# The 1e-9 of a softmax's row sums: one addition becomes a sum over two values, in three fixed tiles

## The chip, the cores and the metric

The kernel runs on one core of one Trainium2 chip. A core has five engines that work side by side, each through its own list of instructions in order: PE (TensorE, matmuls and transposes), DVE (VectorE), ACT (ScalarE), POOL (GpSimd) and SP (which issues most DMA transfers). They wait for each other by semaphores. The metric is the device time of the whole program in microseconds (us); lower is better.

## The reference

Three stages follow each other: attention with normalized queries and keys (4 batches, 12 heads, 448 tokens, head size 64), a mixture of experts in which each of 1792 tokens goes to one of 8 experts, and a dense layer with a sigmoid GELU. The change concerns the end of the softmax alone:

```python
scores = scores - np.max(scores, axis=-1, keepdims=True)
attn = np.exp(scores)
attn = attn / (np.sum(attn, axis=-1, keepdims=True) + 1e-09)
return np.matmul(attn, v).astype(np.float32)
```

## The kernel before

**Attention.** The 48 heads run one after the other, software-pipelined. The 448 tokens of a head are 4 chunks of 112 partitions. `qk` (L218) multiplies two chunks at a time into a PSUM tile `S`; `top` (L229, DVE) takes the negated row maxima into a small tile `sm`; `ex` (L236, ACT) forms the exponentials `A` and, in the same instruction, their row sums, also into `sm`. `at` (L245, PE) transposes `A` into a PSUM tile `pA` with two buffers, which ACT (L252) or DVE (L254) copies out; `avu` (L265, PE) multiplies with V for a pair of heads. The division is done late: `finish_pair` (L274 to L279) copies the product out, adds 1e-9 to the 8 row sums per partition of the pair (L278) and takes their reciprocals `rinv` (L279). One head later `xtok` (L289, PE) transposes the product into the PSUM tile `tp`, of which there is one buffer, and `put_x` (L301, DVE) multiplies it with `rinv`. The transposes of the next queries (L184) and keys (L199) use the same single `tp` buffer, as do the gate's products (L314, L325, read by DVE at L328 and L335).

**The order.** It is written out by hand: the list `ORDER` names the steps of one head, and the scheduler leaves them so. In it `FP` is `finish_pair`, done at every second head as the last step but the gate's, directly before the next head's `top` on DVE; `XP` is `put_x`, at the other heads. `S4` is a step of a weight conversion that runs beside the attention: each step is one DVE instruction (L896 or L901, in turn) with two SBUF inputs, directly ahead of `FP` or `XP`.

**POOL's part.** Once for four heads it prepares queries and keys of a later group: `norm` (12 small operations, L159 to L162, then L164 and two of L167), `split` (L172), and `squares` of the group after (L131 and the foldings L136, L137 for q, then for k). DVE sums what it folded (L142, L146) and gives it the start of the next group's norm (L151).

**After the attention** come the routing, then four pairs of experts, each with its share of the dense layer.

```python
"K0 M0 A0 A1 C1 P3 C0 TQ CQ E0 K1 A2 TK M1 A3 CK C3 C2 AV P0 LK E1 S4 XT P1 P2 FP XP GA GB S5"
```

Of the kernel before, what the change touches and what calls it, by code (L numbers as in the profile page):

```python
# [20 lines left out]
FT = mybir.dt.float32  # L21
# [5 lines left out]
OP = mybir.AluOpType  # L27
AX = mybir.AxisListType
# [23 lines left out]
class Attn:  # L52


    def __init__(s, ctx, tc, q, k, v, g_q, g_k, w_gate, consts, xd, logits):
        s.tc, s.nc = tc, tc.nc
        s.q, s.k, s.v = q, k, v
        s.B, s.H, s.S, s.D = q.shape
        s.C, s.NC = 112, 4
        s.identf, s.identr = consts["identf"], consts["identr"]  # L60
        s.xd, s.logits = xd, logits
        nc = s.nc
        ep = lambda name, bufs=1: ctx.enter_context(tc.tile_pool(name=name, bufs=bufs))
        s.cst = ep("a_cst")
        s.io = ep("a_io", 2)
        s.wk = ep("a_wk", 2)
        s.ps = ctx.enter_context(tc.tile_pool(name="a_ps", bufs=1, space=bass.MemoryType.PSUM))
        s.groups, s.of = [], {}
        for b in range(s.B):
            h = b * s.H  # L70
            for n in ([2, 2, 4, 4] if b == 0 else [4, 4, 4]):
                for i in range(n):
                    s.of[h + i] = (len(s.groups), i)
                s.groups.append((h, n))
                h += n
        s.grp, s.nbuf, s.nsmall = {}, 0, 0
        s.load(0, "qk")
        s.gk = s.cst.tile([128, 2], FT, name="gk")
        for hh in range(2):
            for j, g in enumerate((g_q, g_k)):  # L80
                nc.scalar.dma_start(s.gk[hh * 64:(hh + 1) * 64, j:j + 1],
                                    bass.AP(tensor=g.tensor, offset=g.offset, ap=[[1, 64], [1, 1]]))
        s.load(0, "v")
        s.load(1)
        s.load(2)
        s.wg0 = s.cst.tile([128, 6, 8], FT, name="wg0")
        nc.scalar.dma_start(s.wg0, w_gate.rearrange("(c p) e -> p c e", p=128))
        s.A, s.sums, s.qT, s.khi, s.klo, s.AT, s.xuT, s.rinv, s.av = {}, {}, {}, {}, {}, {}, {}, {}, {}
        s.Sp, s.pA, s.sumsp = {}, {}, {}

    def params(s):
        nc = s.nc
        s.G = s.cst.tile([128, 1], FT, name="G")
        nc.vector.scalar_tensor_tensor(s.G, s.gk[:, 0:1], 1.0 / math.sqrt(s.D), s.gk[:, 1:2],
                                       op0=OP.mult, op1=OP.mult)
# [116 lines left out]
    def qk(s, h, u):  # L212
        nc = s.nc
        p = s.ps.tile([128, 2, 512], FT, name="S", bufs=2)[:112]
        for c in range(2):
            i = 2 * u + c
            for n, mv in enumerate((s.khi[h], s.klo[h])):
                nc.tensor.matmul(p[:, c, 0:448], s.qT[h][:, i, :], mv.rearrange("p i t -> p (i t)"),  # L218
                                 start=(n == 0), stop=(n == 1))
        if u == 0:  # L220
            s.A[h] = s.wk.tile([112, 4, 448], FT, name="A", bufs=2)
            if h % 2 == 0:
                s.sums2 = s.wk.tile([112, 4, 2, 2], FT, name="sm", bufs=3)
                s.sumsp[h // 2] = s.sums2[:, :, 1]
            s.sums[h] = s.sums2[:, :, :, h % 2]
        s.Sp[u] = p

    def top(s, h, u):
# [39 lines left out]
    def finish_pair(s, pr):  # L268
        nc = s.nc
        b, pl = divmod(pr, 6)  # L270
        if pl == 0:
            s.rinv[b] = s.wk.tile([112, 4, 12], FT, name="rinv", bufs=2)
        xu = s.wk.tile([128, 448], FT, name="xu", bufs=5)
        nc.scalar.copy(xu, s.av[pr])  # L274
        s.xuT[pr] = xu
        ri = s.rinv[b]
        o = ri[:, :, 2 * pl:2 * pl + 2]
        nc.vector.tensor_scalar(o, s.sumsp[pr], 1e-9, None, op0=OP.add)  # L278
        nc.vector.reciprocal(o, o)  # L279

    def xtok(s, pr, end=False):
# [1045 lines left out]
```

## Time and profile before

| | us |
|---|---|
| runs shown | 1264.83, 1273.66, 1274.99 (median 1273.66) |
| the profiled execution | 1265.38 |
| its span, first to last instruction | 1263.6 |
| busy: PE, DVE, POOL, ACT | 1141.4, 875.3, 705.1, 659.2 |
| L278, busy in all | 19.4, in 24 instructions |

Busy time is what an engine spends from the start to the end of its instructions; an instruction that is held up after it began counts as busy for the whole of that. The chain of waits follows the work that ended last back from instruction to instruction.

### The profile page before, as it was taken

The page shows a single profiled execution, that of the slowest core. Times are in us where ns is not written, and L with a number is a line of the kernel's source. Part 1 is how long each engine was busy: PE and PEld are TensorE (multiplying, and loading weights), DVE is VectorE, ACT ScalarE, POOL GpSimd, SP SyncE. Part 2 cuts the span into 40 slices and gives each one's busy share as a digit, 9 for nine tenths or more (in the row PEclk, how much of TensorE's full clock was granted, in tenths as well). Part 3 has the DMA queues.
Part 4 walks back from the last instruction along what each step waited for, and adds up shares of the span by engine and source line. Part 5 has one row for each costly group of instructions (what it writes and reads, how often), then busy time and mean ns, then how long its engine had stood idle before and what let it go on. Part 6 is the DMA issues. An engine that isn't in the chain of part 4 may idle for free.

```text
span 1263.6 us, 19388 instructions
## 1 busy us (share of the span) xinstructions
PE 1141.4 (90%) x6952; PEld 961.0 (76%) x6952; DVE 875.3 (69%) x1525; ACT 659.2 (52%) x1289; POOL 705.1 (56%) x588
## 2 busy tenths in 40 slices
PE   4999999999967777879999999999999899999995
PEld 3666666667536676768988898988989799899995
DVE  7799999999789878698657936447885533781100
ACT  4888888888643245654234545224544323555420
POOL 3788677784344546446645674565455355554552
PEclk9899999999967888899998999999999999999998
DMA  6454454423124379864336643436643343763421
GB/s 174 117 145 110 127 152 116 139 76 89 33 74 105 104 206 285 269 220 149 103 110 194 189 127 110 130 106 185 196 130 104 101 124 119 209 190 112 135 78 33
DMA packets 185504, 172.95 MB, mean 137 GB/s; under 512 B 9536, under 2 KB 159808, under 8 KB 185408
## 3 DMA queue, kind: packets, MB, share of 16 engines
q1 hardware_dynamic: 180080, 160.55, 44.0%
q0 software_dynamic: 4224, 11.14, 2.9%
q8 instruction: 55, 0.90, 0.3%
q14 instruction: 41, 0.34, 0.1%
q10 hardware_dynamic: 1104, 0.03, 0.0%
HBM read 147.96 MB, written 23.72 MB: 136 GB/s over the span
## 4 chain that ended last, share of the span: by engine, by line
PE 63%; DVE 23%; issue 6%; DMA 3%; ACT 2%; POOL 2%; SPq 0%; POOLq 0%; DVEq 0%; ACTq 0%
PE mm L1025 11%; PE mm L1026 11%; PE mm L1027 11%; PE mm L1036 5%; PE S L218 5%; PE pA L245 5%; PE av L265 4%; PE mm L1037 3%; DVE gs L1082 2%; DVE B L565 2%; DVE wc L901 2%; DVE B L567 2%; DVE tt L1078 1%; DMA xg<-xd,idx 1%; DVE wc L896 1%
## 5 line engine op out<-in xcount | busy, mean ns | idle before, releaser
L964 POOL TENSOR_TENSOR wlo<-raw,whi 128x768 fp32r<-128x768 f32 (+1 forms) x175 | 385.5, 2205 | 380.9 <-ACT whi L961 362.9
L961 ACT CAST whi<-raw 128x768 fp32r<-128x768 f32 (+1 forms) x224 | 207.0, 924 | 145.6 <-issue 50.8
L1025 PE MATMUL mm<-gs,whi 128*128 128x448 f32 (+1 forms) x432 | 159.4, 369 | 0.5 <-DVE zs L1075 0.5
L1026 PE MATMUL mm<-gs,whi 128*128 128x448 f32 (+1 forms) x432 | 155.9, 361 | 0.0
L1027 PE MATMUL mm<-gs,wlo 128*128 128x448 f32 (+1 forms) x432 | 155.8, 361 | 0.0
L1025 PE MATMUL mm<-zs,whi 128*128 128x448 f32 x384 | 144.1, 375 | 4.6 <-ACT whi L961 4.6
L1027 PE MATMUL mm<-zs,wlo 128*128 128x448 f32 x384 | 142.6, 371 | 5.3 <-POOL wlo L964 3.6
L1026 PE MATMUL mm<-zs,whi 128*128 128x448 f32 x384 | 142.1, 370 | 0.9 <-DVE zs L1084 0.9
L236 ACT ACTIVATE A<-S,sm 112x448 f32<-112x448 f32 x192 | 122.5, 658 | 12.6 <-DVE sm L229 12.6
L1036 PE MATMUL mm<-gs,whi 128*128 128x448 f32 x336 | 110.7, 385 | 10.1 <-DVE gs L1082 10.1
L229 DVE TENSOR_REDUCE sm<-S 112x2 f32<-112x896 f32 x96 | 104.1, 1085 | 19.3 <-PE S L218 18.2
L1036 PE MATMUL mm<-xs,whi 128*128 128x448 f32 x336 | 111.9, 389 | 0.1
L245 PE MATMUL pA<-ident,A 112*112 112x112 f32 x768 | 99.8, 264 | 9.3 <-DVE AT L254 9.1
L245 PEld LDWEIGHTS pA<-ident,A 112*112 112x112 f32 x768 | 84.0, 136 | 22.3 <-DVE AT L254 11.0
L1097 DVE TENSOR_TENSOR gs<-sg,gs 128x448 fp32r<-128x448 f32 x64 | 42.2, 661 | 81.9 <-ACT gs L1096 81.8
L1025 PEld LDWEIGHTS mm<-gs,whi 128*128 128x128 f32 x432 | 83.5, 193 | 10.7 <-issue 4.3
L1095 ACT ACTIVATE sg<-mm 128x448 f32<-128x448 f32 x64 | 34.8, 543 | 103.9 <-PE mm L1027 103.9
L1027 PEld LDWEIGHTS mm<-gs,wlo 128*128 128x128 f32 x432 | 83.4, 193 | 6.2
L1026 PEld LDWEIGHTS mm<-gs,whi 128*128 128x128 f32 x432 | 83.5, 193 | 5.7
L1037 PE MATMUL mm<-xs,wlo 128*128 128x224 f32 x336 | 83.4, 276 | 4.3 <-POOL spacer L1134 1.9
L1037 PE MATMUL mm<-gs,wlo 128*128 128x224 f32 x336 | 83.8, 270 | 1.0 <-DVE wlo L964 1.0
L218 PE MATMUL S<-khi,qT 128*112 128x448 f32 x192 | 79.2, 412 | 4.9 <-ACT khi L206 4.9
(228 smaller groups left out, 2632.6 us busy)
## 6 DMA issues: line engine op xcount, KB each, us to landing
raw<-in_moe_w_dram SPq DMA_DIRECT2D x64, 384.0 KB
raw<-in_moe_w_dram SPq DMA_DIRECT2D x48, 512.0 KB
raw<-din SPq DMA_DIRECT2D x64, 384.0 KB
raw<-dout SPq DMA_DIRECT2D x48, 512.0 KB
r<-in_moe_w_in_dram SPq DMA_DIRECT2D x24, 512.0 KB
r<-in_moe_w_out_dram SPq DMA_DIRECT2D x24, 512.0 KB
din<-wc SPq DMA_DIRECT2D x24, 256.0 KB
dout<-wc SPq DMA_DIRECT2D x48, 128.0 KB
```

Of the source, the lines that this page charges most:

```text
L218: nc.tensor.matmul(p[:, c, 0:448], s.qT[h][:, i, :], mv.rearrange("p i t -> p (i t)"), start=(n == 0), stop=(n == 1))
L229: s.nc.vector.tensor_reduce(s.sums[h][:, 2 * u:2 * u + 2, 0], s.Sp[u][:, :, 0:448], axis=AX.X, op=OP.max, negate=True)
L236: s.nc.scalar.activation(s.A[h][:, i, :], p[:, c, 0:448], AF.Exp, bias=sm[:, i, 0:1], scale=1.0, accum_out=sm[:, i, 1:2])
L245: nc.tensor.transpose(p[:, qc], s.A[h][:, qc, kc * 112:(kc + 1) * 112], s.identf)
L265: nc.tensor.matmul(p[hh * 64:(hh + 1) * 64, :], s.grp[g]["v"][:, hl, kc * 64:(kc + 1) * 64], s.AT[h][:, kc, :], start=(kc == 0), stop=(kc ...
L961: nc.scalar.copy(hi, t)
L964: f = lambda: eng.tensor_tensor(lo, t, hi.bitcast(FT), op=OP.subtract)
L1025: nc.tensor.matmul(p, hi[:, k], x[0], start=first, stop=False)
L1026: nc.tensor.matmul(p, hi[:, k], x[1], start=False, stop=False)
L1027: nc.tensor.matmul(p, lo[:, k], x[0], start=False, stop=last)
L1036: a = lambda: nc.tensor.matmul(p, hi[:, k], x.rearrange("p h t -> p (h t)"), start=first, stop=last)
L1037: b = lambda: nc.tensor.matmul(p[:, 0:224], lo[:, k], x[:, 0], start=False, stop=False)
```

## The change

Three tiles of 112 partitions by 4 chunks by 2 heads by 3 values are made once, in a pool that is never recycled, in place of a rotating tile with three buffers. The three values are the negated maximum, the row sum and a constant 1e-9, which POOL writes once at the start. Pairs of heads use the three tiles in turn. In `finish_pair` a sum over the last two values takes the place of the addition of 1e-9; it reads 16 values per partition and writes the same 8.

```diff
         s.Sp, s.pA, s.sumsp = {}, {}, {}
 
+        s.sm = [s.cst.tile([112, 4, 2, 3], FT, name="sm%d" % i) for i in range(3)]
+        for t in s.sm:
+            nc.gpsimd.memset(t[:, :, :, 2:3], 1e-9)
+
...
             if h % 2 == 0:
-                s.sums2 = s.wk.tile([112, 4, 2, 2], FT, name="sm", bufs=3)
-                s.sumsp[h // 2] = s.sums2[:, :, 1]
-            s.sums[h] = s.sums2[:, :, :, h % 2]
+                s.sums2 = s.sm[h // 2 % 3]
+                s.sumsp[h // 2] = s.sums2[:, :, :, 1:3]
+            s.sums[h] = s.sums2[:, :, h % 2, :]
...
         o = ri[:, :, 2 * pl:2 * pl + 2]
-        nc.vector.tensor_scalar(o, s.sumsp[pr], 1e-9, None, op0=OP.add)
+        nc.vector.tensor_reduce(o, s.sumsp[pr], axis=AX.X, op=OP.add)
         nc.vector.reciprocal(o, o)
```

The order on DVE around the second pair's `finish_pair`, before (a number behind a name tells tiles apart):

```order
L210 SCALAR_TENSOR_TENSOR klo<-tp,G,khi 128x448
L901 SCALAR_TENSOR_TENSOR wc<-wab,wc 128x512
L278 TENSOR_SCALAR rinv<-sm 112x4x2
L279 RECIPROCAL rinv<-rinv 112x4x2
L229 TENSOR_REDUCE sm<-S 112x2
L254 COPY AT<-pA 112x448
L229 TENSOR_REDUCE sm<-S 112x2
L254 COPY AT<-pA 112x448
L210 SCALAR_TENSOR_TENSOR klo<-tp,G,khi 128x448
L896 SCALAR_TENSOR_TENSOR wc<-wab,wc 128x512
L142 TENSOR_REDUCE ms<-hq 112x16
L301 TENSOR_TENSOR xt<-tp,rinv 112x512
```

The same place now (lines from L91 on stand four lower in the file):

```order
L214 SCALAR_TENSOR_TENSOR klo<-tp,G,khi 128x448
L905 SCALAR_TENSOR_TENSOR wc<-wab,wc 128x512
L282 TENSOR_REDUCE rinv<-sm_116 112x4x2
L283 RECIPROCAL rinv<-rinv 112x4x2
L233 TENSOR_REDUCE sm_115<-S 112x2
L258 COPY AT<-pA 112x448
L233 TENSOR_REDUCE sm_115<-S 112x2
L258 COPY AT<-pA 112x448
L214 SCALAR_TENSOR_TENSOR klo<-tp,G,khi 128x448
L900 SCALAR_TENSOR_TENSOR wc<-wab,wc 128x512
L146 TENSOR_REDUCE ms<-hq 112x16
L305 TENSOR_TENSOR xt<-tp,rinv 112x512
```

One operation is another, and nothing has moved. The waits on semaphores are the same on all engines, too.

POOL's start, with the three new instructions behind the first table of indices:

```order
L1263 IOTA jp 128x128
L93 MEMSET sm_115 112x8
L93 MEMSET sm_116 112x8
L93 MEMSET sm_117 112x8
L483 IOTA ii 112x112
L487 IOTA ii 112x224
```

They stand ahead of the tables (`ii`) that DVE takes up in its first microseconds.

## Rows read from the trace of the kernel before

**Rows 1.** Busy by stretch: us, engines' busy (x instructions), PE clock, DMA share, GB/s.

```profile
54.00:290.00 236.00, 222.41 (x1561) 157.07 (x1559) 224.38 (x311) 198.22 (x498) 178.29 (x198) 1.00 0.46 123
```

**Rows 2.** The chain of waits between 54 and 304 us, shares by line.

```profile
by line: PE S L218 19.8%; PE pA L245 17.8%; PE av L265 15.9%; DVE wc L901 6.7%; DVE rinv L278 6.5%; DVE AT L254 4.5%; PE tp L184 4.5%; PE tp L199 4.3%; DVE sm L229 4.1%; DVE klo L210 3.6%; PE tp L289 3.5%; DVE wc L896 3.4%; PE tp L314 2.1%;
```

**Rows 3.** Line L278: durations in ns as min/median/max, first and last start.

```profile
L278 DVE TENSOR_SCALAR rinv<-sm x24: 155/166/1861, 54.0 to 341.5; 112x8 f32<-112x8 f32 x24
```

**Rows 4.** Timeline from 64 us: start, duration, instruction, [idle before it, releaser].

```profile
64.86 2.12 DVE L901 SCALAR_TENSOR_TENSOR wc<-wab,wc 128x512 int32<-128x512 int32 x1
...
66.39 2.34 POOL L131 TENSOR_TENSOR sq<-qt 112x1024 f32<-112x1024 f32 x1
...
66.90 1.86 DVE L278 TENSOR_SCALAR rinv<-sm 112x8 f32<-112x8 f32 x1
...
68.91 1.04 DVE L229 TENSOR_REDUCE sm<-S 112x2 f32<-112x896 f32 x1
...
70.54 0.60 PE L245 MATMUL pA<-ident,A 112*112 112x112 f32 x4 [1.48 <-DVE AT L254]
...
70.83 1.89 POOL L131 TENSOR_TENSOR sk<-kt 112x1024 f32<-112x1024 f32 x1
...
72.55 0.72 DVE L896 SCALAR_TENSOR_TENSOR wc<-wab,wc 128x512 int32<-128x512 int32 x1
...
72.80 1.63 POOL L136 TENSOR_TENSOR hk<-sk 112x512 f32<-112x512 f32 x1
...
73.19 0.41 DVE L142 TENSOR_REDUCE ms<-hq 112x16 f32<-112x256 f32 x1
...
73.52 0.67 DVE L301 TENSOR_TENSOR xt<-tp,rinv 112x512 f32<-112x512 f32 x1
...
74.71 0.52 PE L184 MATMUL tp<-identr,qp 112*128 112x112 f32 x4
```

**Rows 5.** Timeline, the last of the nine long L278.

```profile
277.40 1.86 DVE L278 TENSOR_SCALAR rinv<-sm 112x8 f32<-112x8 f32 x1
```

**Rows 6.** What PE waited for between 54 and 304 us: us, times, longest.

```profile
PE tp L184 <- DVE prod L328: 6.8, 5, 1.4
PE pA L245 <- DVE AT L254: 6.4, 6, 1.5
```

**Rows 7.** What POOL waited for between 54 and 304 us.

```profile
POOL rw L159 <- DVE rinv L278: 54.8, 10, 7.5
```

**Rows 8.** Line L142, the reduction of POOL's folded squares.

```profile
L142 DVE TENSOR_REDUCE ms<-hq x10: 405/406/409, 46.7 to 285.1; 112x16 f32<-112x256 f32 x10
```

**Rows 9.** Groups of instructions: two other reductions, busy us and mean ns.

```profile
L229 DVE TENSOR_REDUCE sm<-S 112x2 f32<-112x896 f32 x96 | 104.1, 1085 | 19.3 <-PE S L218 18.2
...
L628 DVE TENSOR_REDUCE mx<-t 112x1 f32<-112x8 f32 x8 | 1.3, 162 | 0.3
```

**Rows 10.** Timeline from 118 us, where the gate's first half follows L278.

```profile
118.47 1.86 DVE L278 TENSOR_SCALAR rinv<-sm 112x8 f32<-112x8 f32 x1
...
121.00 0.50 PE L184 MATMUL tp<-identr,qp 112*128 112x112 f32 x4 [1.39 <-DVE prod L328]
...
122.44 1.89 POOL L131 TENSOR_TENSOR sk<-kt 112x1024 f32<-112x1024 f32 x1
...
124.41 1.29 POOL L136 TENSOR_TENSOR hk<-sk 112x512 f32<-112x512 f32 x1
...
124.55 1.70 DVE L896 SCALAR_TENSOR_TENSOR wc<-wab,wc 128x512 int32<-128x512 int32 x1
```

**Rows 11.** Timeline from 145 us, where its second half follows.

```profile
145.23 1.85 DVE L278 TENSOR_SCALAR rinv<-sm 112x8 f32<-112x8 f32 x1
...
147.63 0.50 PE L184 MATMUL tp<-identr,qp 112*128 112x112 f32 x4 [1.31 <-DVE prod L328]
...
149.97 0.60 PE L245 MATMUL pA<-ident,A 112*112 112x112 f32 x4 [0.20 <-DVE AT L254]
...
151.98 1.03 DVE L896 SCALAR_TENSOR_TENSOR wc<-wab,wc 128x512 int32<-128x512 int32 x1
```

**Rows 12.** Timeline of the first 12 us: MEMSETs of POOL and what DVE takes up.

```profile
0.25 0.10 POOL L1311 MEMSET const-float32-0.0<- 128x1 f32 x1 [0.25 <-issue]
...
0.28 0.11 POOL L1311 MEMSET const-float32-1.0<- 128x1 f32 x1
...
1.06 0.21 POOL L479 IOTA ii<- 112x112 int32 x1
...
1.52 0.21 DVE L480 TENSOR_SCALAR before<-ii 112x112 f32<-112x112 int32 x1
...
11.25 0.25 POOL L100 MEMSET wgb<- 128x192 f32 x1
```

## The prediction

> **What bounds the kernel now.** I began with the busy times by stretch. From 54 to 290 us, the attention's steady part, PE is busy 222.4 of 236 us at a granted clock of 1.00 and DVE 224.4 [rows 1]: two engines are nearly full, so a stall on either can set the pace. The chain of waits for 54 to 304 us says which: mostly PE lines, but 6.5% lies on L278, which is 16.3 us of 250 for an instruction that handles 8 values per partition [rows 2]. The line's own durations explain it: the median is 166 ns, the longest 1861 ns [rows 3]. So I read the timeline around a long one. L278 starts at 66.90, POOL's L131 has been running since 66.39 and ends at 68.73, and L278 ends at 68.76 [rows 4]. It waits out a POOL instruction that has nothing to do with its data. No semaphore is named there, and its time counts as busy. All 24 took 19.4 us by the groups of instructions; 9 of them are long, the first at 66.90 and the last at 277.40 [rows 4, 5], one for each group of four heads that POOL prepares. All nine sit behind the same POOL operation. Each of the nine costs about 1.86 - 0.17 = 1.69 us, in all 15.2 us of DVE time.
>
> Does the stall reach PE? Behind the long L278, DVE's L229 starts at 68.91, the copy L254 comes after it, and PE, which needs that copy's buffer, stands still for 1.48 us until 70.54 [rows 4]. Over 54 to 304 us PE waited 6.4 us for L254 and 6.8 us for L328, a gate product that also stands behind L278 [rows 6]. Those 13.2 us are what PE can win back here.
>
> **Does the new operation wait as well?** The trace has reductions that read SBUF on DVE while POOL works. L142 starts at 73.19 in the middle of POOL's L136 (72.80 to 74.43) and takes 0.41 us [rows 4]; all ten instances lie between 405 and 409 ns [rows 8]. So a reduction does not wait for POOL. The Trainium skill, page "SBUF — State Buffer", section "Who interferes with whom", has it so: VectorE and GpSimd share a pair of ports that an instruction holds to its end, a tensor_scalar can enter a mode that takes the pair, and a tensor_reduce on this chip never does. The long L278 and the steady L142 agree with it.
>
> **What the new operation costs.** It reads 16 values. L628 reads 8 in 162 ns [rows 9], L142 reads 256 in 406 ns [rows 8]; 16 is next to the former, so I take 0.17 us, the same as a short L278. The bounds are 0.16 and 0.41 us. The other 15 instructions thus change by 0, at most 15 x 0.24 = 3.6 us. The Trainium skill, page "VectorE: DVE Perf Modes", section "Rules for kernel authors", speaks against the change: a tensor_reduce on a hot path is called the slowest DVE operation. At 16 values the rows leave no room for that; by its letter the slower rival below would be the forecast.
>
> **Where the time comes back, group by group.** A DVE instruction with two SBUF inputs waits for POOL too: L901 took 2.12 us and L896 took 1.70 us where 0.72 is enough [rows 4, 10]. The next of them after L278 is L896 of the following head, and POOL works without a pause from its norm to the end of its foldings. So an earlier DVE can run into an earlier POOL operation. The nine cases are of three kinds.
>
> Four without a gate (66.90 is the first). L901 ends at 66.98, so L278 is done at 67.15 and not 68.76, 1.61 us sooner; the wait of 1.48 us on PE goes [rows 4]. L896 would come at 72.55 - 1.48 = 71.07. There POOL's L131 for k runs from 70.83 to 72.72, and L896 can only get through at its end, about 72.57: it ends at 73.27 as it does today. L301 behind it still frees `tp` at 74.19. PE's L184 needs that buffer; it ran at 74.71, is now ready at 73.23 and starts at 74.24. So 0.47 us remain of 1.48 [rows 4]. 4 x 0.47 = 1.9 us.
>
> Three with the gate's first half (118.47). PE's wait of 1.39 us at 121.00 goes. L896 today ends at 126.25, behind POOL's L136 (124.41 to 125.70). Coming at 124.55 - 1.39 = 123.16 it falls into POOL's L131 (122.44 to 124.33) instead and gets through before L136, at about 124.2, ending near 124.9: 1.38 us sooner, in step with PE [rows 10]. 3 x 1.39 = 4.2 us.
>
> Two with the second half (145.23). PE's waits of 1.31 and 0.20 us go; L896, now at 151.98 with 1.03 us, moves ahead of L136 in the same way and keeps up [rows 11]. 2 x 1.51 = 3.0 us.
>
> In all 1.9 + 4.2 + 3.0 = 9.1 us. POOL does not stand in the way: ten times it waits for DVE, 54.8 us in all [rows 7], so it starts each group earlier when DVE does, and the pattern repeats. The bounds are 13.2 us, if no later L896 gives anything back, and 15.2 us if every microsecond of DVE counts; below, 0.
>
> **The rest of the edit.** Three MEMSETs on POOL ahead of L479, on the way to DVE's first instructions. The small ones start 0.03 us apart and take 0.10 us, the large one 0.25; L479 ends at 1.27 and L480 starts at 1.52, so 0.25 us are free [rows 12]. I take 0.1 us, between 0 and 0.5 (3 x 0.25 less the 0.25). The fixed tiles change no wait: a pair's tile is written again three pairs later, two heads after L278 read it. Routing and experts follow the attention in order and only shift.
>
> Sum: -9.1 + 0.1 = -9.0 us. Against the profiled execution that is 1265.38 - 9.0 = 1256.4 us; against the median of the runs shown, 1273.66 - 9.0 = 1264.7. The four times known stand two near 1265 and two near 1274, so I take the middle of the two sums, **1260 us**.
>
> **Rivals.**
> - Everything comes back: L896 slips in ahead of POOL's L131 for k, or `tp` is not needed so soon. It needs L896 at 71.07 to be before 70.83, only 0.24 us off, which speaks for it. 13.2 to 15.2 us, so 1250 to 1261 against the two levels. Chance 0.20.
> - Nothing comes: the reduction waits for POOL as the addition did (L142's ten even times speak against it), or the experts' stage, with its own collisions of DVE and POOL, takes up the shift. 0 us: 1265 to 1274. Chance 0.16.
> - Slower: the reduction over short, spaced pairs is dear. It stands in front of L229, on which the exponentials hang, 24 times. With L229's own 1.085 us [rows 9] it adds 24 x (1.085 - 0.17) = 22 us, and 22 - 9 = 13 us slower, 1278 to 1287. It decides against the change from 0.17 + 9.0 / 24 = 0.55 us on; L142 needs 0.41 us for sixteen times the values. Chance 0.04.
> - The forecast, 6 to 12 us: 0.60.
>
> **How the numbers follow.** The range runs from all of the gain on the lower level, 1250, to little gain on the upper, 1272; the ends are 1249 and 1272. About 1%, 12.7 us, is what a measurement here can tell from no change. My sum is under it: "same" takes most of the forecast and the rival without gain. "Faster" takes most of the first rival and the edge of the forecast, since the times differ by 10 us among themselves: 0.30. "Slower" takes the third and a little of that spread: 0.05. "Same" is 0.65.
>
> **What would show it.** In the profile after, line L282 with 24 instructions between 160 and 200 ns and none near 1.8 us; its share gone from the chain of waits. PE's waits for L258 and L332 in this stretch down from 13.2 us to a few. In the groups without a gate L900 (the old L896) at about 2.2 us where 0.72 stood, and a new wait of PE's L188 for L305, about 1 us, four times; in the gate's groups L900 ending ahead of POOL's hk folding. If L900 stays at 0.7 there, the first rival holds; if L282 has a maximum near 1.8 us, the second; if its median is over 0.5 us, the third. The sum would be wrong if the time after 342 us changed its length by more than a few us.

## The result, and the profile after

The changed kernel takes 1256.39 us (median of 4 runs, 1253.94 to 1258.48) against 1271.14 us (4 runs of the kernel before, 1264.83 to 1274.99). The ratio is 0.9884 with a 95% interval of 0.9855 to 0.9914: 14.7 us faster, and between 10.9 and 18.4 by the interval. The profiled execution has a span of 1256.2 us, 7.4 less than the one before.

Line L282, the old L278, as min/median/max in ns; it answers to [rows 3]:

```profile
L282 DVE TENSOR_REDUCE rinv<-sm x24: 155/160/165, 57.1 to 330.9; 112x8 f32<-112x16 f32 x24
```

None of the 24 is long. Busy time in the attention's steady part, to be held against [rows 1]:

```profile
54.00:290.00 236.00, 235.01 (x1652) 166.25 (x1651) 222.61 (x332) 211.03 (x528) 187.47 (x213) 1.00 0.47 125
```

PE (the first pair of numbers) is busy 235.0 of 236 us where it was 222.4, and it gets 1652 instructions done there and not 1561. The view of waits shows no line for PE between 54 and 304 us, where [rows 6] had 13.2 us. POOL still waits for DVE, for 43.1 us and not 54.8 [rows 7]:

```profile
POOL rw L163 <- DVE rinv L282: 43.1, 10, 10.5
```

The chain of waits for that stretch, which answers to [rows 2]:

```profile
by line: PE S L222 24.6%; PE av L269 20.9%; PE pA L249 19.8%; DVE wc L900 5.8%; PE tp L188 5.1%; PE tp L203 4.9%; DVE sm L233 3.9%; PE tp L293 3.0%; DVE AT L258 2.3%; PE tp L318 2.1%; DVE klo L214 1.7%; DVE xt L305 1.7%; DVE wc L905 1.2%; P
```

The 6.5% of L278 are gone. Now the place of [rows 4], a group without a gate (start, duration, instruction):

```profile
68.04 2.13 DVE L905 SCALAR_TENSOR_TENSOR wc<-wab,wc 128x512 int32<-128x512 int32 x1
...
69.59 2.34 POOL L135 TENSOR_TENSOR sq<-qt 112x1024 f32<-112x1024 f32 x1
...
70.09 0.16 DVE L282 TENSOR_REDUCE rinv<-sm 112x8 f32<-112x16 f32 x1
...
70.41 1.04 DVE L233 TENSOR_REDUCE sm<-S 112x2 f32<-112x896 f32 x1
...
72.05 0.57 PE L249 MATMUL pA<-ident,A 112*112 112x112 f32 x4
...
74.04 0.68 DVE L900 SCALAR_TENSOR_TENSOR wc<-wab,wc 128x512 int32<-128x512 int32 x1
74.05 2.42 POOL L135 TENSOR_TENSOR sk<-kt 112x1024 f32<-112x1024 f32 x1
...
74.97 0.68 DVE L305 TENSOR_TENSOR xt<-tp,rinv 112x512 f32<-112x512 f32 x1
```

L282 runs inside POOL's L135 (69.59 to 71.93) without a delay, and PE's L249 has no wait in front of it. The prediction had L900 arrive behind POOL's L135 for k and wait. It starts 0.01 us ahead of it, takes 0.68 us, and POOL's instruction is the one that grows, from 1.89 to 2.42 us. In the three other groups without a gate the trace gives both the same start, with the same outcome, here the second group:

```profile
98.16 0.68 DVE L900 SCALAR_TENSOR_TENSOR wc<-wab,wc 128x512 int32<-128x512 int32 x1
98.16 2.44 POOL L135 TENSOR_TENSOR sk<-kt 112x1024 f32<-112x1024 f32 x1
```

In the group with the gate's first half, which answers to [rows 10], it is as predicted:

```profile
118.33 0.16 DVE L282 TENSOR_REDUCE rinv<-sm 112x8 f32<-112x16 f32 x1
...
118.64 0.37 DVE L332 TENSOR_TENSOR prod<-tp,rinv 112x256 f32<-112x256 f32 x1
...
119.22 0.52 PE L188 MATMUL tp<-identr,qp 112*128 112x112 f32 x4
...
122.29 1.90 POOL L135 TENSOR_TENSOR sk<-kt 112x1024 f32<-112x1024 f32 x1
...
122.79 1.95 DVE L900 SCALAR_TENSOR_TENSOR wc<-wab,wc 128x512 int32<-128x512 int32 x1
...
124.27 1.60 POOL L140 TENSOR_TENSOR hk<-sk 112x512 f32<-112x512 f32 x1
```

L900 falls into POOL's L135 for k (122.29 to 124.19), ends at 124.74 and is through in front of L140, as the prediction had it.

**Where the time went, by stretch.** The starts of L278 or L282 divide every profile in three: up to the first of them, from the first to the last, and from there to the end of the span. Executions profiled, in us (the last two experiments, which move other work, follow in the text):

| kernel | to the first | first to last | the rest |
|---|---|---|---|
| before | 54.0 | 287.5 | 922.1 |
| before, again | 56.1 | 287.5 | 918.3 |
| tiles alone | 57.4 | 287.7 | 925.7 |
| two tensors added | 53.9 | 287.5 | 921.7 |
| changed | 57.1 | 273.8 | 925.3 |
| changed, again | 56.2 | 273.7 | 921.5 |
| no constant | 57.3 | 273.5 | 923.2 |
| reduction twice | 54.0 | 278.8 | 926.1 |

The middle column repeats to 0.3 us and follows the edit: the change gives 13.7 to 13.8 us there. The outer two vary by 3.5 and by 8 us without regard to it, the kernel before itself by 2.1 and 3.8. So the two first profiles differ by 7.4 us only because the changed one lost 3.1 us before the first L282 and 3.2 after the last; the medians above do not hang on one execution.

### The profile page after: what moved, and what is told of

It is laid out like the page before. It is cut to its first block, busy times and chain, and to the rows that moved or that the text cites. A ratio compares the mean times of both kernels' runs of the same rounds, so it can differ in the third digit from the quotient of the medians.

```text
span 1256.2 us, 19391 instructions
## 1 busy us (share of the span) xinstructions
PE 1147.1 (91%) x6952; PEld 965.6 (77%) x6952; DVE 854.4 (68%) x1525; ACT 659.2 (52%) x1289; POOL 703.8 (56%) x591
## 4 chain that ended last, share of the span: by engine, by line
PE 67%; DVE 19%; DMA 5%; issue 5%; ACT 2%; POOL 1%; SPq 0%; POOLq 0%; DVEq 0%; ACTq 0%
PE mm L1029 12%; PE mm L1031 12%; PE mm L1030 12%; PE S L222 6%; PE mm L1040 5%; PE av L269 5%; PE pA L249 5%; PE mm L1041 3%; DMA dout<-wc 2%; DVE gs L1086 2%; DVE wc L900 2%; DVE B L571 2%; DVE tt L1082 2%; DMA xg<-xd,idx 1%; DVE B L569 1%
## 5 line engine op out<-in xcount | busy, mean ns | idle before, releaser
L249 PE MATMUL pA<-ident,A 112*112 112x112 f32 x768 | 100.9, 266 | 2.6 <-DVE AT L258 2.4
L249 PEld LDWEIGHTS pA<-ident,A 112*112 112x112 f32 x768 | 85.1, 137 | 14.9 <-DVE AT L258 3.6
L1031 PEld LDWEIGHTS mm<-zs,wlo 128*128 128x128 f32 x384 | 73.8, 192 | 15.1 <-POOL wlo L968 5.2
```

The source lines that it names most:

```text
L249: nc.tensor.transpose(p[:, qc], s.A[h][:, qc, kc * 112:(kc + 1) * 112], s.identf)
L1031: nc.tensor.matmul(p, lo[:, k], x[0], start=False, stop=last)
```

## The experiments

**The changed kernel once more.**

> The changed kernel once more, to learn how much of its profile repeats. If the gain is the nine waits of the addition, attention from 70 to 290 us repeats: L282 24 times at 155 to 165 ns, L900 at 0.68 us in the four groups without a gate. The stretch from 12 to 54 us lost 3.2 us in the first profile; if that was chance (PE clock) it will differ here, if it belongs to the change (new MEMSETs, shifted start) the first L282 will again start near 57.1 us. Ratio to before 0.985 to 0.992.

Measured: 1254.85 us (4 runs) against 1270.61 (25 runs of the kernel before), ratio 0.9896 (0.985 to 0.9943). L282 takes 153 to 164 ns, L900 takes 0.68 us in all four groups without a gate, and the first to last is 273.7 us. The first L282 starts at 56.2, so a late start alone does not yet look like chance. The kernels "two tensors added" and "reduction twice" have the same MEMSETs and start it at 53.9 and 54.0; the kernel before, without them, started at 54.0 and 56.1. The new MEMSETs are not the reason. What differs is the granted clock of PE and one collision. The stretches 30 to 36 and 42 to 48 us in the first profile of the kernel before:

```profile
30.00:36.00 6.00, 4.57 (x24) 3.94 (x25) 4.43 (x7) 4.09 (x9) 5.81 (x4) 0.76 0.36 140
42.00:48.00 6.00, 6.00 (x40) 4.43 (x39) 4.14 (x6) 4.50 (x12) 4.51 (x4) 0.89 1.00 263
```

and in the first profile of the changed kernel:

```profile
30.00:36.00 6.00, 4.86 (x21) 4.11 (x22) 4.55 (x8) 3.24 (x7) 5.54 (x3) 0.57 0.46 161
42.00:48.00 6.00, 5.53 (x24) 4.86 (x25) 3.14 (x5) 3.50 (x10) 4.59 (x4) 0.51 1.05 262
```

The share near the end of each row is the clock: 0.76 and 0.89 against 0.57 and 0.51, close to the lower of the two levels (1.2 of 2.4 GHz). Between the two stretches, from 36 to 42 us, PE was busy 3.89 us before and 3.24 us after, at 0.78 in both. In the profile after, the first conversion step (38.95 us) also met POOL's L135 and took 1.87 us instead of 0.70. The other rows of the table show that this does not come from the edit, for either form falls into each case: with a clock of 0.82 to 0.89 from 42 to 48 us the first start is 53.9 to 54.0 (before, two tensors added, reduction twice), with 0.72 it is 56.1 and 56.2 (before again, changed again), with 0.50 and 0.51 it is 57.1 to 57.4 (changed, tiles alone, no constant). Whether the clock makes the late start or follows from it, and why it differs, stays open.

**The tiles without the sum.**

```diff
-        nc.vector.tensor_reduce(o, s.sumsp[pr], axis=AX.X, op=OP.add)
+        nc.vector.tensor_scalar(o, s.sumsp[pr][:, :, :, 0], 1e-9, None, op0=OP.add)
```

> The three fixed tiles and the MEMSETs stay, the sum over two values is an addition again. Theory (the addition waits for POOL's running operation, the tiles do nothing): nine L282 near 1.86 us again, PE's waits in 54 to 304 us back at about 13 us, time as before (ratio 0.997 to 1.003). Rival (the gain is from tiles that are never recycled): L282 short, time as the changed kernel, ratio about 0.988.

Measured: ratio 1.0007 (0.9975 to 1.0039), and first to last 287.7 us.

```profile
L282 DVE TENSOR_SCALAR rinv<-sm x24: 155/167/1859, 57.4 to 345.1; 112x8 f32<-112x8 f32 x24
```

The nine long ones are back, with the tiles and MEMSETs in place. PE's waits are those of [rows 6] to the tenth of a microsecond, 6.8 and 6.4. The tiles alone give nothing.

**Two tensors added.**

```diff
-        nc.vector.tensor_reduce(o, s.sumsp[pr], axis=AX.X, op=OP.add)
+        nc.vector.tensor_tensor(o, s.sumsp[pr][:, :, :, 0], s.sumsp[pr][:, :, :, 1], op=OP.add)
```

> The 1e-9 of the fixed tiles is added by an operation on two tensors in SBUF instead of a reduction. Theory (what matters is whether the DVE operation takes a second way into SBUF that POOL holds, and L896 and L901 with two SBUF inputs show that they do): nine long ones near 1.86 us return, time as before, ratio 0.997 to 1.003. Rival (only the addition of a constant waits, any sum of two stored values escapes): L282 at 0.16 us throughout, ratio about 0.988.

Measured: ratio 1.0012 (0.9983 to 1.0041), first to last 287.5 us.

```profile
L282 DVE TENSOR_TENSOR rinv<-sm x24: 154/166/1858, 53.9 to 341.4; 112x8 f32<-112x8 f32 x24
```

The same 16 values are read and the same 8 written as by the reduction, in 166 ns when nothing is in the way. Yet this form waits for POOL, nine times again, and the reduction does not. So it is the form of the operation that decides, not its data and not its length.

**No constant.**

```diff
-        nc.vector.tensor_scalar(o, s.sumsp[pr], 1e-9, None, op0=OP.add)
-        nc.vector.reciprocal(o, o)
+        nc.vector.reciprocal(o, s.sumsp[pr])
```

> The kernel before with the addition taken out: the reciprocal reads the row sums itself, and the 1e-9 is left out of the computation. Theory (only the addition's wait cost time): the reciprocal L278 stays at about 0.2 us, 24 times, as it did beside POOL before, and the stretch from the first to the last is that of the changed kernel, 273.7 us, or up to 1 us less for the missing instruction; ratio 0.985 to 0.993. Rival (whatever DVE issues at this place waits for POOL): nine reciprocals near 1.9 us, ratio 0.997 to 1.003.

Measured: 1257.33 us (4 runs), ratio 0.9899 (0.9839 to 0.9959), first to last 273.5 us.

```profile
L278 DVE RECIPROCAL rinv<-sm x24: 186/194/198, 57.3 to 330.8; 112x8 f32<-112x8 f32 x24
```

A reciprocal in the very place of the addition, with the rotating tiles, does not wait: nine of the 24 start inside POOL's L131 for q, as the long additions did, and none takes over 198 ns. So a short instruction in this place costs next to nothing (this kernel saves one, and its stretch is 0.2 us under the changed kernel's); one that waits cost 13.7 us.

**The reduction twice, in the four groups without a gate.**

```diff
         nc.vector.tensor_reduce(o, s.sumsp[pr], axis=AX.X, op=OP.add)
+        if pr in (1, 3, 9, 15):
+            nc.vector.tensor_reduce(o, s.sumsp[pr], axis=AX.X, op=OP.add)
         nc.vector.reciprocal(o, o)
```

> The changed kernel with the reduction done twice, one after the other, in the four pairs without a gate whose addition used to be long (pairs 1, 3, 9, 15): some 0.2 us more on DVE in each. Theory (there the conversion's L900 now gets in 0.01 to 0.05 us ahead of POOL's L135 for k, and the prediction's give-back is what happens when it does not): four times L901 (the old L900) goes from 0.68 to some 2.3 us, the pair's group is 1.0 to 1.3 us longer, 4 to 5 us in all. Rival (there is slack, nothing is that close): L901 stays at 0.68 us and the whole costs 0 to 0.8 us.

Measured: 1261.68 us (10 runs), ratio 0.9955 (0.9925 to 0.9985), first to last 278.8 us, 5.1 us more than the changed kernel for four instructions of 0.17 us. The old L896 and L901 are L902 and L907 here, `put_x` is L307:

```profile
66.92 0.16 DVE L282 TENSOR_REDUCE rinv<-sm 112x8 f32<-112x16 f32 x1
67.11 0.17 DVE L284 TENSOR_REDUCE rinv<-sm 112x8 f32<-112x16 f32 x1
...
70.86 1.91 POOL L135 TENSOR_TENSOR sk<-kt 112x1024 f32<-112x1024 f32 x1
71.07 2.25 DVE L902 SCALAR_TENSOR_TENSOR wc<-wab,wc 128x512 int32<-128x512 int32 x1
...
73.56 0.68 DVE L307 TENSOR_TENSOR xt<-tp,rinv 112x512 f32<-112x512 f32 x1
...
74.30 0.52 PE L188 MATMUL tp<-identr,qp 112*128 112x112 f32 x4 [0.83 <-DVE xt L307]
```

What PE waited for between 54 and 304 us:

```profile
PE tp L188 <- DVE xt L307: 3.3, 4, 0.8
```

L902 comes 0.21 us behind POOL's L135, waits it out, and L307 frees the `tp` buffer late: the chain that the prediction wrote for these groups, with L902 even at the time it named, 71.07. (The text of the expectation calls that instruction L901; in this kernel it is L902, the old L896, which is L900 in the changed kernel.)

**The kernel before, once more.** The edit is four empty lines.

> The kernel before once more, with four empty lines in its file, for what of its profile repeats: from the first L282 (old L278) to the last 287.5 us, nine long ones. Before the first and after the last it may differ by 3 to 4 us each way, if those two stretches are chance and not the change.

Measured: 1263.68 us, one execution; first to last 287.5 us; 2.1 us later at the first L282 and 3.8 us less after the last than the other profile of this kernel. It is the second row of the table above and shows how far the outer columns differ between two executions of one program.

**The conversion's steps moved, twice.** Can the remaining waits be taken away, too?

```diff
-            if 0 <= h < 46:
-                for _ in range(SLOT_CONVERT[h % 2].count(at)):
+            if 0 <= h < 46 and at == 4:
+                for _ in range((2, 0, 0, 2)[h % 4]):
```

> The changed kernel with the conversion's steps taken out of the two heads in which POOL runs its long operations and put, two at a time, into the two others of each four. Theory (DVE's two-input steps still wait 1.3 to 2.3 us for POOL in those heads, and hold PE up a little): their long ones go, and the stretch from the first to the last L282 falls from 273.7 to about 270 us, 0.2 to 0.4 us for each group. Rival (PE is now the bound, these waits are covered): 273 to 275 us, no change; with two steps in a row it may be a little longer.

Measured: 1265.39 us (10 runs), ratio 0.9953 (0.9923 to 0.9983), first to last 288.0 us: a miss.

```profile
70.40 0.88 DVE L900 SCALAR_TENSOR_TENSOR wc<-wab,wc 128x512 int32<-128x512 int32 x1
...
70.69 2.35 POOL L135 TENSOR_TENSOR sk<-kt 112x1024 f32<-112x1024 f32 x1
...
71.32 2.27 DVE L905 SCALAR_TENSOR_TENSOR wc<-wab,wc 128x512 int32<-128x512 int32 x1
...
73.12 1.59 POOL L140 TENSOR_TENSOR hk<-sk 112x512 f32<-112x512 f32 x1
...
73.84 0.68 DVE L305 TENSOR_TENSOR xt<-tp,rinv 112x512 f32<-112x512 f32 x1
...
74.57 0.52 PE L188 MATMUL tp<-identr,qp 112*128 112x112 f32 x4 [1.37 <-DVE xt L305]
```

The last of each four heads (`h % 4 == 3`) is not free of POOL's long operations. Two steps there mean that the second meets L135, and L305 with the single `tp` buffer stands behind it; PE waited 13.1 us for L305, nine times, about as much as the change had won. The second try moved one step only:

```diff
-    "K0 M0 A0 A1 C1 P3 C0 TQ CQ E0 K1 A2 TK M1 A3 CK C3 C2 AV P0 LK E1 S4 XT P1 P2 FP XP GA GB S5").split()
+    "K0 M0 A0 A1 C1 P3 C0 TQ CQ E0 S6 K1 A2 TK M1 A3 CK C3 C2 AV P0 LK E1 S4 XT P1 P2 FP XP GA GB S5").split()
...
-                for _ in range(SLOT_CONVERT[h % 2].count(at)):
+                for _ in range((at == 6) if h % 4 == 1 and h > 1 else 2 * (at == 4) if h == 4 else (at == 4)):
```

> The changed kernel with one of the four conversion steps of a group moved: in the head in which POOL works through its 12 small operations, the step (now the second half of a piece, which gives ACT nothing to do) runs between that head's first copy L258 and its second L233, ahead of POOL's long ones. Theory (that step waited some 1.3 us for POOL and held PE's L188 up by some 0.35 us through the single tp buffer, and DVE has 0.2 to 0.7 us free before the second L233): that step takes 0.7 to 1 us, from the first to the last L282 some 271 us instead of 273.7, 2 to 3 us less. Rival (the step delays the second L233 and the exponentials instead, or shifts the next head so that L905 loses its lead over POOL's L135): 273 to 279 us.

Measured: 1253.81 us (4 runs), ratio 0.9875 (0.983 to 0.992); from the first L282 (57.8) to the last (337.3) 279.5 us. The step itself is down to 0.68 us as the theory had it, but the groups are longer by 0.4 to 0.6 us (71.19 to 95.76 is 24.57 us, against 24.12), and the stretch is 5.7 us longer than the changed kernel's, just past the rival's 273 to 279 us. The view of waits has 4.1 us for PE between 54 and 304 us, on five lines, where the changed kernel has none; which of the rival's two ways led there was not followed up. Its rest is 911.9 us, 6 to 14 less than in any row of the table. This kernel does one conversion step more during the attention and the experts' stage orders its work by what is left; that this makes the difference was not tested. By the times it cannot be told from the changed kernel.

## Why the prediction was right or wrong

Rows for what follows: starts of further long L278 before, the weight load for PE's L245 of [rows 4], and starts of L282 after.

```profile
92.70 1.86 DVE L278 TENSOR_SCALAR rinv<-sm 112x8 f32<-112x8 f32 x1
...
172.13 1.86 DVE L278 TENSOR_SCALAR rinv<-sm 112x8 f32<-112x8 f32 x1
...
70.54 0.38 PEld L245 LDWEIGHTS pA<-ident,A 112*112 112x112 f32 x4 [1.69 <-DVE AT L254]
...
94.21 0.16 DVE L282 TENSOR_REDUCE rinv<-sm 112x8 f32<-112x16 f32 x1
...
143.73 0.16 DVE L282 TENSOR_REDUCE rinv<-sm 112x8 f32<-112x16 f32 x1
...
169.15 0.15 DVE L282 TENSOR_REDUCE rinv<-sm 112x8 f32<-112x16 f32 x1
```

- **The cause of the gain: right.** The long additions wait for a POOL operation with which they share no data, and a reduction does not. Taking the operation back (tiles alone) undoes the whole gain; another form that waits (two tensors) gives nothing; one that does not wait (reciprocal) gives all. The Trainium skill, "SBUF — State Buffer", section "Who interferes with whom", says that a tensor_scalar in a two-port mode and an operation with two SBUF inputs contend with GpSimd and a tensor_reduce does not; these traces agree in all three (1859, 1858 and 165 ns at most). That the addition ran in such a mode is the page's reading; no view here names a mode.
- **The price of the reduction: right.** 0.17 us was taken and 0.160 measured, under the addition's 0.166. The slower rival had its point at 0.55 us. The Trainium skill's rule in "VectorE: DVE Perf Modes", "Rules for kernel authors", that a tensor_reduce on a hot path is the slowest operation, does not hold at 16 values.
- **The MEMSETs: right.** DVE's L164 (now L168) of the first microseconds starts at 9.83 us and not 9.72: 0.11 us, where 0.1 was taken.
- **The groups with a gate: right.** The distance from one long L278 to the next fell from 26.76 to 25.40 us with the first half (1.36, forecast 1.39), and from 26.90 to 25.42 with the second (1.48, forecast 1.51).
- **The groups without a gate: wrong.** "So 0.47 us remain of 1.48" was the step; the distance fell from 25.80 to 24.12 us, by 1.68. The error is in "L896 would come at 72.55 - 1.48 = 71.07". I took PE's idle time as the limit of what DVE gains, and I let L278 begin at the end of L901 (66.98), although its row has it start at 66.90; so I had 1.61 us where the row gives 1.86 - 0.16 = 1.70. DVE moves by that much: L229 stood at 68.91 and comes 1.70 us sooner (70.41 after, less the 3.20 us by which POOL's L131 of that place is later, is 67.21), so L896 comes at 70.85, where POOL's L135 for k starts. In the trace the two start within 0.01 us of each other, in all four groups, and L900 is not held up. PE's start moves by 1.69 as well (72.05 less 3.20 is 68.85, against 70.54), although its row shows an idle time of 1.48: the profile's ends of matmuls are modelled, and the row counts from such an end. The row of the weight load at the same place has the 1.69. The first rival, which named this edge as 0.24 us off, is what happened in these four groups. The kernel with the reduction twice puts 0.2 us back and has the forecast's case: its groups fall from 25.80 to 25.40 us, 0.40 where 0.47 was forecast, and the stretch gains 8.7 us in all, where 9.1 was forecast.
- **The sum.** 4 x 1.68 + 3 x 1.36 + 2 x 1.48 = 13.8 us, where 9.1 was forecast; it is the band of the first rival, 13.2 to 15.2 us, to which 0.20 was given, and outside the forecast's 6 to 12 us. That the time lies inside the stated 1249 to 1272 us does not bear the sum out. That the measured median, 1256.39, is the 1256.4 worked out from the profiled execution is an accident: a gain too small by 4.7 us was taken from a time that was 5.8 us under the median of the kernel before. The "two levels" do not show in more runs: 25 runs of the kernel before spread from 1262 to 1276 with a median of 1270.6.
- **The sizes.** The measured 1.16% lies over the 1% that the prediction set for "faster", to which it gave 0.30; the interval, 0.86 to 1.45%, has that bound inside it. With the edge read rightly the sum would have been 13.7 us, 1.08% of the 1273.66 taken there, and "faster" at least as likely as "same".

## What to carry to other kernels

An instruction whose shortest and longest durations differ tenfold on the same shape (here 155 and 1861 ns) is probably waiting, and its wait stands in the busy column; look at what the neighbouring engine runs from its start to its end, and find a form of the operation that does not wait. When a stall goes, replay the engine that was stalled by its own rows and not by the idle time of the one that waited for it. Where the next contender arrives within a few tenths of a microsecond of the other engine's start, give both outcomes the same weight, and price both: here 0.2 us decided over 5 us.

## What the runs showed that I had not expected

- A shift of 0.2 us decides who waits. The changed kernel's two profiles and that of "one step moved" hold twelve conversion steps that start between 0.01 us ahead of POOL's L135 for k and 0.01 us behind it: each takes 0.68 us, POOL's L135 takes 2.42 to 2.45 us instead of 1.89, and in the changed kernel PE shows no wait. In "reduction twice" four start 0.20 to 0.21 us behind: the step takes 2.23 to 2.25 us, and PE waits up to 0.83. The edge lies between; in [rows 10] a step 0.14 us behind L136 already waits (1.70 us).
- The steady stretch of 273 to 288 us repeats to 0.3 us between executions, while the 54 us ahead of it, where PE's granted clock goes between 0.5 and 1.0, vary by 3.5 us.
